# Transposes of split weights in high and low halves, other engines for the rests, and another order of the work

## The chip, the cores and the metric

The kernel runs on one core of one Trainium2 chip. The metric is the device time of one execution in microseconds (us); a time "before" is the median of several runs of the unchanged kernel. One further execution was profiled, and the rows in this document come from it.

The core has a tensor engine (TensorE, PE in the rows; PEld is its weight load), VectorE (DVE), ScalarE (ACT), GpSimd (POOL) and SyncE (SP), which here only issues DMAs. Each engine works through its own instructions in the order of the program and waits at semaphores for the others.

## The reference

Stage 1 is attention over a window of 64 positions; stage 2 is a mixture of four experts, each a causal attention, of which every position uses two:

```python
# stage 1: batch 8, 8 heads, 576 positions, 64 columns a head
scores = scale * np.matmul(q, k.transpose(0, 1, 3, 2))
mask = (rel >= 0) & (rel < 64)
attn = softmax(np.where(mask, scores, -1e9))      # sum + 1e-9 below the line
x = concat_heads(np.matmul(attn, v))              # 8 x 576 x 512
# stage 2: 4 experts, 64 columns each, the 2 largest logits a position
logits = x @ w_gate
for e in range(4):
    q, k, v = x @ wq[e], x @ wk[e], x @ wv[e]
    a = softmax(causal(scale * (q @ k.transpose(0, 2, 1))))
    out += chosen_weight[e] * (a @ v @ wo[e])
```

## The kernel before

Everything is float32 at the ends and is computed with numbers split into a high and a low part, so that the products of the parts keep the accuracy.

**Stage 1** goes over 72 groups of four tiles: scores (`s1_mm`, m in the order), mask and softmax (`s1_qk`, q; the norms are GpSimd's line 338), transposes on TensorE (`s1_t`, t; line 361) and products with v (`s1_av`, a).

**Stage 2** goes over the eight batches b and, in each, over two pairs pr of experts. Per batch: values (`s2_v`, v: the result is split into three bf16 parts `V2`, the second and third made from a rest by two GpSimd instructions each, lines 510 and 511), gate (`s2_gate`, g) and output (`s2_o`, o). Per (b, pr): projections (`s2_k`, k; `s2_q`, r), scores (`s2_mm`, x, line 601), softmax (`s2_soft`, y), and then the part that the change is about:

- `s2_w` (u, lines 645 to 670) makes nine rows of weights, row x belonging to block (x+1)//2 of the causal pattern: 64, 192, 192, 320, 320, 448, 448, 576 and 576 columns. ACT writes the high part in f16 (line 663). The low part is the rest: by one VectorE instruction (line 666) or by two GpSimd instructions, multiply and subtract (lines 668, 669). `LOW` says which: rows 0 to 6 by GpSimd and rows 7 and 8 by VectorE; in the last pair (7,1) `LAST` gives all to VectorE. `u..0` has rows 0 to 6, `u..1` rows 7 and 8.
- `s2_turn` (D, line 678) turns the split weights by a DMA transpose from the source tile `SPLIT` (sp) to `TURN` (tu), issued by SP. k = 0 takes blocks 0 to 2 (22 tiles of 128 x 128, "blocks" in what follows of a DMA's size), k = 1 block 3 (16), k = 2 block 4 (20). High and low parts lie together and go in one DMA. Blocks 3 and 4 share `SPLIT[1]`: block 4 is written when block 3 has been read; in between GpSimd clears a strip of it (line 480).
- `s2_av` (A, line 701) multiplies the turned weights with `V2`: part 0 (k = 0) in 50 matmuls, part 1 (k = 1 and 2) in 60, for each piece of the pattern the five products of parts one behind the other: three with the high weights, two with the low ones. ACT and VectorE split the result into `YH` and `YL` (lines 708, 710), from which `s2_o` makes the output.

**The order** is written out by hand: the string `ORDER` lists the units; each naming runs the unit to its next `yield`, and the digits behind a colon are the PSUM banks it takes. Each engine receives its instructions in that order and keeps it. SP thus issues loads (p and h), transposes (D) and stores (the last step of o) in one queue: a transpose that waits for its weights holds all that stand behind it.

A unit is named with its indices: D712 is batch 7, pair 1, k = 2; A710 is batch 7, pair 1, part 0. The last pair stands like this in the order (`...` leaves out):

```python
... x710:31 x710 k711 k711 x712:46 x712 x711:27 x711 u701
... D702 D702 o54 o54 o60 o60 u710 u710 u710 ... y713 y713 y713
u711 o61:7 A700:2 o62:4 A701:6 o61 o63:5 o62 D710 D710 D711 D711 o61 o61 o62 o62 u711 A710:3 A710 u711 u711
u711 u711 u711 o63 A701 A700 A701 A710 A710 A700 A700 o71:1 o70:7 D712 D712 ... A711:4 A711 A711 o72:5 ...
```

Of the kernel before, what the change touches and what calls it, by code (L numbers as in the profile page):

```python
# [30 lines left out]
LOW = "PPPPPPPDD"  # L31
LAST = "DDDDDDDDD"
# [127 lines left out]
def window_attention_moe_attention(ctx: ExitStack, tc: tile.TileContext, qT, kT, vW,  # L160
# [264 lines left out]
    def place(i, e, low):  # L425

        if i == 0:
            return 0, low, low
        n = i + 1
        at = (0, 2, 10, 0, 0)[i] + n * (2 * low + e)  # L430
        return int(i > 2), at, at + (16 if i == 4 else 0)

# [409 lines left out]
```

## Time and profile before

| what | value |
|---|---|
| median of 3 runs | 504.77 us (503.76 to 505.1) |
| profiled execution, whole time | 502.08 us |
| its span, first to last instruction | 500.4 us |
| instructions | 16956 |
| TensorE busy | 445.5 us (89%), 6192 matmuls |
| VectorE busy | 418.4 us (84%) |
| ScalarE busy | 356.5 us (71%) |
| GpSimd busy | 303.6 us (61%) |
| transposes `tu<-sp` | 48, median 5.7 us from issue to landing |

The time is the whole execution's, the span what lies between its first and last instruction; rows count from the span's start. A share of busy time says how much of a stretch an engine worked, and nothing on what it waited for: that is told by the number in brackets behind a row (idle time ahead of it, and what ended it) and by the chain of waits, which follows the work that ended last back to the start. "To landing" is the time from a DMA's issue to the semaphore that tells of its end.

### The profile page before, as it was taken

How to read it: one execution, taken by the hardware profiler on the slowest of the kernel's cores; microseconds unless marked ns; L12 is line 12 of the kernel's file. 1: busy time of each engine (PE TensorE's matmuls, PEld its weight loads, DVE VectorE, ACT ScalarE, POOL GpSimd, SP SyncE). 2: the span in 40 equal slices, each digit the busy share in tenths (PEclk: the TensorE clock that was granted, in tenths of full speed). 3: DMA queues.
4: the chain of work that ended last, by engine and by line, in shares of the span. 5: the costliest groups of instructions: out<-in, count | busy, mean ns of one | idle time of the engine just before them, and what ended most of it. 6: DMA issues, size and time to landing. Idle time of an engine off the chain costs nothing.

```text
span 500.4 us, 16956 instructions
## 1 busy us (share of the span) xinstructions
PE 445.5 (89%) x6192; PEld 395.2 (79%) x6192; DVE 418.4 (84%) x1788; ACT 356.5 (71%) x1304; POOL 303.6 (61%) x663
## 2 busy tenths in 40 slices
PE   7999998797899797999789899989999989978846
PEld 6788888686798676978689888879888879967735
DVE  5879999898799997989979999989999896882720
ACT  6987997486775676768877588758696677574642
POOL 6987597767474763574748364967659364764000
PEclk9999999999899998999989999998999989998979
DMA  8954373849895597095976679494996675466684
GB/s 270 372 215 149 101 203 94 162 92 198 173 162 160 124 222 256 1 224 121 210 229 127 169 175 184 128 153 96 270 193 125 169 122 102 78 141 125 144 162 141
DMA packets 141251, 81.85 MB, mean 164 GB/s; under 512 B 123120, under 2 KB 124144, under 8 KB 141168
## 3 DMA queue, kind: packets, MB, share of 16 engines
q1 hardware_dynamic: 141088, 80.63, 68.7%
q8 instruction: 49, 0.80, 0.7%
q14 instruction: 34, 0.28, 0.2%
q10 hardware_dynamic: 80, 0.13, 0.1%
HBM read 40.90 MB, written 9.44 MB: 101 GB/s over the span
## 4 chain that ended last, share of the span: by engine, by line
DVE 34%; DMA 22%; PE 16%; POOL 12%; ACT 9%; issue 6%; SPq 1%; POOLq 0%; DVEq 0%; ACTq 0%
DMA tu<-sp 18%; DVE p L616 6%; DVE pt L375 5%; DVE sm L314 4%; POOL p L338 4%; PE ps L701 4%; ACT sm L325 4%; DVE sp L666 2%; PE ps L487 2%; DVE p L322 2%; DMA k<-in_kT_dram 2%; PE ps L601 2%; PE ps L488 2%; PE ps L489 2%; ACT sp L663 2%
## 5 line engine op out<-in xcount | busy, mean ns | idle before, releaser
L338 POOL TENSOR_SCALAR p<-p,st 128x64 f32<-128x64 f32 x216 | 73.0, 361 | 40.0 <-DVE st L334 20.1
L663 ACT ACTIVATE sp<-p,r 128x576 f16<-128x576 f32 (+3 forms) x128 | 72.3, 607 | 31.4 <-DMA tu<-sp 22.1
L620 ACT ACTIVATE p<-p,r 128x192 f32<-128x192 f32 (+3 forms) x128 | 77.2, 606 | 19.9 <-DVE r L616 14.7
L325 ACT ACTIVATE p<-p,st 128x64 f32<-128x64 f32 x216 | 72.3, 338 | 10.7 <-DVE p L322 8.4
L701 PEld LDWEIGHTS <-v 128*64 128x64 bf16 x1760 | 61.0, 113 | 22.6 <-issue 13.2
L701 PE MATMUL ps<-tu,v 128*64 128x64 f16 (+2 forms) x1760 | 64.0, 232 | 16.6 <-DMA tu<-sp 9.6
L375 DVE TENSOR_TENSOR pt<-ps,tri 64x512 f32<-64x512 f32 (+1 forms) x120 | 75.4, 632 | 3.5 <-PE ps L361 1.8
L669 POOL TENSOR_TENSOR sp<-p,sp 128x192 f16<-128x192 f32 (+2 forms) x90 | 72.3, 804 | 7.5
L616 DVE CUSTOM_DVE_ANT_0 p<-ps,causal 128x320 f32<-128x320 f32 (+3 forms) x160 | 67.9, 469 | 4.3 <-PE ps L601 2.5
L314 DVE CUSTOM_DVE_ANT_0 sm<-ps,win 128x128 f32<-128x128 f32 x264 | 61.8, 281 | 5.9 <-PE ps L297 4.9
L601 PE MATMUL ps<-kt,qt 64*128 64x256 f32 (+2 forms) x480 | 50.5, 333 | 6.5 <-DVE kt L571 2.0
L668 POOL TENSOR_SCALAR p<-p,r 128x192 f32<-128x192 f32 (+2 forms) x90 | 51.4, 571 | 4.7 <-ACT sp L663 4.7
L297 PE MATMUL ps<-k,q 64*64 64x128 f32 (+1 forms) x1080 | 41.6, 279 | 8.6 <-DMA k<-in_kT_dram 6.1
L601 PEld LDWEIGHTS ps<-kt,qt 64*128 64x128 f32 x480 | 36.9, 190 | 13.4 <-DVE kt L571 2.5
L388 PE MATMUL ps<-pt,v 128*64 128x64 f32 x1080 | 38.7, 226 | 5.3 <-DMA v<-in_vW_dram 2.5
L297 PEld LDWEIGHTS ps<-k,q 64*64 64x64 f32 x1080 | 31.8, 137 | 14.4 <-issue 4.8
L487 PE MATMUL ps<-xh,wqhi 128*128 128x320 f32 (+1 forms) x128 | 40.2, 314 | 2.8 <-ACT out L178 1.1
L388 PEld LDWEIGHTS ps<-pt,v 128*64 128x64 f32 x1080 | 34.5, 139 | 10.2 <-DMA v<-in_vW_dram 2.8
L325 ACT ACTIVATION_READ_ACCUMULATOR p<-p,st 128x1 f32 x216 | 41.2, 191 | 0.0
L480 POOL MEMSET sp<- 128x256 f16 (+1 forms) x35 | 10.7, 309 | 49.6 <-DMA tu<-sp 43.5
L487 PE MATMUL ps<-xh,wkhi 128*128 128x256 f32 (+1 forms) x128 | 39.7, 310 | 0.9 <-DVE kt L571 0.8
L666 DVE SCALAR_TENSOR_TENSOR sp<-p,r,sp 128x576 f16<-128x576 f32 (+3 forms) x38 | 31.0, 830 | 11.1 <-ACT sp L663 10.8
(138 smaller groups left out, 1283.8 us busy)
## 6 DMA issues: line engine op xcount, KB each, us to landing
v<-in_vW_dram SPq DMA_DIRECT2D x30, 576.0 KB, 4.9
k<-in_kT_dram SPq DMA_DIRECT2D x29, 320.0 KB, 4.4
q<-in_qT_dram SPq DMA_DIRECT2D x29, 288.0 KB, 4.1
out_dram<-out SPq DMA_DIRECT2D x32, 256.0 KB, 3.9
out_dram<-out SPq DMA_DIRECT2D x7, 128.0 KB, 2.5
tu<-sp SPq DMA_TRANSPOSE x48, 5.7
sp<-in_kT_dram SPq DMA_DIRECT2D x2, 320.0 KB, 6.4
p<-in_qT_dram SPq DMA_DIRECT2D x2, 288.0 KB, 5.7
```

Of the source, the lines that this page charges most:

```text
L297: nc.tensor.matmul(S1[g][i][o:o + 64, c:], lhsT=q_t[r, 64 * b:64 * b + 64], rhs=k_t[r, 64 * b + c:64 * b + 128], start=True, stop=True)
L314: nc.vector.tensor_tensor_reduce(out=to, in0=ps[i][:, c:], in1=win[:, int(b == 0), c:], scale=-0.125, scalar=3.0e38, op0=OP.add, op1=OP.mi ...
L325: nc.scalar.activation(pt[:, i], pt[:, i], AF.Exp, bias=st[:, 0, z + i:z + i + 1], scale=-1.0, accum_out=st[:, 1, z + i:z + i + 1])
L338: nc.gpsimd.tensor_scalar(p, p, st[:, 2, i:i + 1], 1.0, op0=OP.mult, op1=OP.mult)
L375: nc.vector.tensor_mul(t[64 * w:64 * w + 64, :n, e], ps[r, :n], tri[r, w, None, :].to_broadcast([64, n, 128]))
L388: nc.tensor.matmul(o[64 * h:64 * h + 64, 4 * x + i], lhsT=pairs[p][2][:, h, b], rhs=t[:, i, c:c + 64], start=True, stop=True)
L487: nc.tensor.matmul(ps, lhsT=ah, rhs=bh, start=first, stop=False)
L601: nc.tensor.matmul(ps[e][:, at(i):at(i) + n], lhsT=QT[pr][r, w, q], rhs=KT[b, pr][r, m, key:key + n], start=x == 0, stop=x == 2)
L616: nc.vector.tensor_tensor_reduce(out=dst, in0=src, in1=mask, scale=1.0, scalar=3.0e38, op0=OP.add, op1=OP.min, accum_out=to)
L620: nc.scalar.activation(p, p, AF.Exp, bias=r2[:, 0, x:x + 1], scale=-1.0, accum_out=r2[:, 1, x:x + 1])
L663: nc.scalar.activation(hi, p, AF.Copy, scale=by)
L701: nc.tensor.matmul(to, lhsT=V2[b % 2][:, c, a, 2 * pr + h], rhs=rhs, start=n == 0, stop=n == len(work_list) - 1, skip_group_check=True)
```

## The change

`ORDER` is replaced as a whole, and six places of the code with it:

1. A turn becomes two DMAs, one for the high and one for the low part: D gets a fourth index (0 high, 1 low), `place` lays all high parts of a turn side by side and all low parts behind them, and sizes halve to 11, 8 and 10 blocks.
2. `s2_av` goes over the five products outside and over the pieces of the pattern inside: all products with high weights come first.
3. Rows 7 and 8 get their rests from GpSimd too; from (6,1) on, so in (6,1), (7,0) and (7,1), VectorE makes all nine.
4. The second and third parts of `V2` of the last batch are made by VectorE.
5. `clear_split` follows the new places.
6. The units get another order and other banks.

```diff
-LOW = "PPPPPPPDD"
-LAST = "DDDDDDDDD"
+LOW = "PPPPPPPPP"
+LATE = (6, 1)
...
     def place(i, e, low):
-        if i == 0:
-            return 0, low, low
-        n = i + 1
-        at = (0, 2, 10, 0, 0)[i] + n * (2 * low + e)
-        return int(i > 2), at, at + (16 if i == 4 else 0)
+        if i < 3:
+            at = 11 * low + (0, 1 + 2 * e, 5 + 3 * e)[i]
+            return 0, at, at
+        at = 2 * low * (i + 1) + e * (i + 1)
+        return 1, at, at + (16 if i == 4 else 0)
...
     def clear_split(i):
-        x, at, _ = place(i, 0, 0)
-        n, c = (4, i + 1) if i else (2, 1)
-        t = SPLIT[x].bitcast(F16)[:, 128 * at:128 * (at + n * c)].rearrange("r (a c) -> r a c", a=n)
-        nc.gpsimd.memset(t[:, :, 128 * c - 64:], 0.0)
+        for low in range(1 if i > 2 else 2):
+            x, at, _ = place(i, 0, low)
+            n, c = (1 if i == 0 else 2 if i < 3 else 4), i + 1
+            t = SPLIT[x].bitcast(F16)[:, 128 * at:128 * (at + n * c)].rearrange("r (a c) -> r a c", a=n)
+            nc.gpsimd.memset(t[:, :, 128 * c - 64:], 0.0)
...
-            nc.gpsimd.tensor_scalar(dst[1], rest, 1.0, 1.0, op0=OP.mult, op1=OP.mult)
-            nc.gpsimd.tensor_tensor(dst[2], rest, dst[1], op=OP.subtract)
+            engine = nc.vector if b == NB - 1 else nc.gpsimd
+            engine.tensor_scalar(dst[1], rest, 1.0, 1.0, op0=OP.mult, op1=OP.mult)
+            engine.tensor_tensor(dst[2], rest, dst[1], op=OP.subtract)
...
-            if (LAST if (b, pr) == (NB - 1, 1) else LOW)[x] == "D":
+            if LOW[x] == "D" or (b, pr) >= LATE:
                 nc.vector.scalar_tensor_tensor(lo, p, by, hi, op0=OP.mult, op1=OP.subtract)
...
-    def s2_turn(b, pr, k):
-        n = (22, 16, 20)[k]
-        src = SPLIT[int(k > 0)].bitcast(F16)[:, 0:128 * n]
-        at = (0, 0, 16)[k]
-        to = TURN[int(k > 0)].bitcast(F16)[:, 128 * at:128 * (at + n)]
-        nc.sync.dma_start_transpose(to.rearrange("r (a c) -> r a c", a=n), src)
+    def s2_turn(b, pr, k, low):
+        n = (11, 8, 10)[k]
+        x, at, to = place((0, 3, 4)[k], 0, low)
+        src, dst = (t[x].bitcast(F16)[:, 128 * a:128 * (a + n)] for t, a in ((SPLIT, at), (TURN, to)))
+        nc.sync.dma_start_transpose(dst.rearrange("r (a c) -> r a c", a=n), src)
...
-        work_list = [(c, blocks, q, q0, a, low) for c, blocks, q, q0 in AVS[part] for a, low in PRODUCTS]
+        work_list = [(c, blocks, q, q0, a, low) for a, low in PRODUCTS for c, blocks, q, q0 in AVS[part]]
```

The end of the new order, from the stretch of batch 6's last transposes on (`...` leaves out; a transpose is named twice, its second naming does nothing):

```python
... y700 A600 ... A601:6 D6110 D6110 D6111 D6111 D6101 D6101 x701:13 x701
... k710:5 r710:4 o53:2 r711:3 ... x702:17 x702 ... D6120 D6120 ... A610:2 D6121
D6121 x703:17 x703 x710:45 x710 o54:3 ... D7000 D7000 A611:1 ... k711:7 k711 ... o60:2 ... D7001 D7001
x712:34 x712 k711 k711 x711:57 x711 y711 D7010 D7010 D7011 D7011 u701 ...
D7020 D7020 D7021 D7021 x713:27 x713 o63:5 o61:1 o62:6 y711 y711 u710 u710 u710 u710 u710 u710 u710 u710
u710 o61 u710 u710 u710 u710 A700:1 y712 y712 y713 A701:3 o61 o61 D7101 D7101 u710 o62 u710
y713 y713 D7110 D7110 u711 u710 u710 D7111 D7111 u711 u711 A700 u711 u711 D7100 D7100 A701 A701 A700 A700
A701 A701 A701 u711 u711 D7120 D7120 D7121 D7121 o62 o62 A710:6 A710 o63 A710 A710 o70:4 ... o71:2 ... A711:7 ...
```

## Rows read from the trace of the kernel before

**Rows 1.** The page: busy us (share of the span) and instructions of an engine.
```profile
PE 445.5 (89%) x6192; PEld 395.2 (79%) x6192; DVE 418.4 (84%) x1788; ACT 356.5 (71%) x1304; POOL 303.6 (61%) x663
```

**Rows 2.** Stretches: length, busy us (instructions) of PE, PEld, DVE, ACT, POOL; clock, DMA.
```profile
60.00:440.00 380.00, 346.61 (x4869) 311.32 (x4865) 344.31 (x1409) 274.99 (x1012) 246.52 (x523) 0.98 0.71 157
440.00:462.00 22.00, 17.22 (x185) 15.21 (x183) 11.82 (x47) 13.24 (x37) 11.97 (x20) 0.92 0.59 123
462.00:500.40 38.40, 26.33 (x314) 20.98 (x312) 14.42 (x48) 17.90 (x45) 0.93 (x3) 0.88 0.65 150
484.00:488.00 4.00, 3.60 (x8) 2.65 (x9) 1.42 (x5) 0.57 (x3) 0.00 (x0) 0.50 0.68 130
492.00:496.00 4.00, 4.00 (x24) 3.44 (x22) 0.58 (x2) 1.39 (x4) 0.00 (x0) 1.00 0.22 81
350.00:375.00 25.00, 24.27 (x377) 21.33 (x374) 24.53 (x103) 19.71 (x72) 14.35 (x31) 1.00 1.00 234
400.00:425.00 25.00, 23.42 (x250) 21.76 (x249) 19.60 (x74) 17.98 (x57) 13.77 (x27) 0.93 0.63 112
```

**Rows 3.** The chain of waits from 440 us on: its shares by engine and line.
```profile
by line: DMA tu<-sp 44.9%; PE ps L701 12.5%; issue 6.1%; DVE sp L666 4.8%; DMA out_dram<-out 3.3%; DVE p L616 3.0%; PE ps L487 2.9%; ACT sp L663 2.3%; PE ps L488 2.0%; PE ps L489 1.9%; PE ps L601 1.7%; POOL px L668 1.2%; POOL sp L669 1.2%; 
```

**Rows 4.** Pieces of that chain: start us, length us, what.
```profile
439.92 4.25 DMA tu<-sp
...
472.66 7.29 DMA tu<-sp
...
484.38 4.86 DMA tu<-sp
```

**Rows 5.** SP's transposes: two timeline rows, all 48 (ns), and the landing of D711.
```profile
472.66 3.63 SPq L678 DMA_TRANSPOSE tu<-sp  x1
...
476.45 2.98 SPq L678 DMA_TRANSPOSE tu<-sp  x1
...
L678 SPq DMA_TRANSPOSE tu<-sp x48: 1317/3275/8168, 69.9 to 484.4; - x48
...
DMA to landing us min/median/max: 5.1/5.1/5.1
```

**Rows 6.** Timeline from 462 us: start, length, engine, line, operation, shapes [idle before <-releaser].
```profile
462.06 2.10 PE L601 MATMUL ps<-kt,qt 64*128 64x256 f32 x24
...
472.57 2.42 PE L701 MATMUL ps<-tu,v 128*64 128x256 f16 x60 [1.43 <-DMA tu<-sp]
...
479.99 1.53 PE L701 MATMUL ps<-tu,v 128*64 128x256 f16 x50 [3.40 <-DMA tu<-sp]
484.40 0.80 PE L487 MATMUL ps<-wohi,yh 128*128 128x512 f32 x1 [2.88 <-ACT yh L708]
...
489.28 2.42 PE L701 MATMUL ps<-tu,v 128*64 128x256 f16 x60
...
472.46 1.23 ACT L663 ACTIVATE sp<-p,r 128x448 f16<-128x448 f32 x2 [1.07 <-DMA tu<-sp]
...
470.16 1.81 DVE L666 SCALAR_TENSOR_TENSOR sp<-p,r,sp 128x192 f16<-128x192 f32 x4
```

**Rows 7.** Groups by line and shape: xcount | busy us, mean ns of one | idle before.
```profile
L669 POOL TENSOR_TENSOR sp<-p,sp 128x448 f16<-128x448 f32 x30 | 31.3, 1045 | 2.5
...
L666 DVE SCALAR_TENSOR_TENSOR sp<-p,r,sp 128x576 f16<-128x576 f32 x32 | 27.9, 883 | 9.8 <-ACT sp L663 9.6
...
L669 POOL TENSOR_TENSOR sp<-p,sp 128x320 f16<-128x320 f32 x30 | 24.4, 813 | 2.5
...
L668 POOL TENSOR_SCALAR p<-p,r 128x448 f32<-128x448 f32 x30 | 19.9, 663 | 2.1 <-ACT sp L663 2.1
...
L668 POOL TENSOR_SCALAR p<-p,r 128x320 f32<-128x320 f32 x30 | 16.6, 553 | 1.3 <-ACT sp L663 1.3
```

**Rows 8.** Waits: who for whom, us in total, times, longest.
```profile
POOL sp L480 <- DMA tu<-sp: 43.5, 12, 8.8
...
PE ps L361 <- POOL p L338: 3.6, 5, 1.4
```

More of the change, by code (lines that the diff above doesn't have):

```diff
@@ L777, in window_attention_moe_attention @@
             for k in range(3):
-                unit(f"D{b}{pr}{k}", s2_turn, b, pr, k)
+                for low in range(2):
+                    unit(f"D{b}{pr}{k}{low}", s2_turn, b, pr, k, low)
             for k in range(4):
```

240 rows, old and new, of the table ORDER are left out of this document.

## The prediction

> **What bounds the kernel now.** I read the busy shares first: TensorE is busy 445.5 of 500.4 us, VectorE 418.4 [rows 1], two engines close together. An average hides stages, so the second view is busy time by stretch [rows 2]. From 60 to 440 us TensorE (346.6 of 380 us) and VectorE (344.3) are tied, each free for a tenth of the time, and GpSimd has room (246.5). After 440 us this is over: from there to 462 TensorE works 17.2 of 22 us, and in the last 38.4 us, from the scores of the last head pair on, it works 26.3, so 12.1 us hold no matmul. Third, the chain of waits over that last stage: 44.9% of it is the transposes that turn the split weights (`tu<-sp`), against 12.5% for the products that use them [rows 3]. So the end of the kernel is a latency chain, the middle is a contest of TensorE and VectorE, and the change touches both.
>
> The chain at the end, in order of time: D710 is issued at 472.66 and holds SP's queue for 3.63 us; D711 behind it goes out at 476.45 and lands 5.1 us later, at about 481.5 [rows 4, 5]. Block 4 shares its source tile with block 3, so its parts wait for that landing; D712 goes out at 484.38 and lands at 489.24 [rows 4]. TensorE meanwhile waits 1.43, 3.40 and 2.88 us [rows 6]. Behind these waits the granted clock is 0.50, the lower of its two levels, from 484 to 488 us; from 492 us on, with matmuls back to back, it is 1.00 [rows 2].
>
> **The halves of the transposes.** The 48 DMAs become 96, over the same bytes. D611, of 16 blocks, lands after 4.25 us, D712, of 20, after 4.86 us [rows 4]: 0.15 us a block, and 1.85 us that do not depend on size. By that line a half of 8, 10 or 11 blocks lands after 3.05, 3.35 or 3.5 us. No row shows a half; the bounds are half of the 16-block landing (2.1 us) and all of it (4.25 us), and I take the line, since both its points are undisturbed issues and the nearer is only 1.5 times larger. On SP's queue the shortest of the 48 took 1.32 us, the median 3.275, and D711 2.98 [rows 5]; a half should not cost more than the shortest whole one, and I take 1.3, between 0.7 and 2.0 us: 96 of them hold SP for 125 us, where 48 at the median hold it for 157. The size-free part overlaps when two are issued back to back: D710 landed at 479.95, and D711, issued 3.8 us after it, 1.6 us later [rows 4, 5].
>
> The Trainium skill, DMA: Bandwidth & Descriptors, section "Anatomy of one DMA", gives every transfer a fixed cost of about 2.0 us, and its rules for kernel authors tell you to coalesce small transfers. The trace agrees on the fixed part (1.85 us); were the 48 added DMAs to pay those 2.0 us one after another, the sum would lose 96 us, and the overlap just shown speaks against that.
>
> What is moved: behind a transpose that waits in SP's queue stand the loads of later pairs and the stores of outputs, and a low half now waits there as a whole one did before. In the order as written the two halves mostly stand together, and in the last pair the low half D7101 even stands ahead of D7110 and D7100. The gain is therefore that each part is short, that block 4's first high part can be written once block 3's high parts have been read, and that the products wait in the order high, low.
>
> **The last 38 us.** I take the trace's own clock as a ruler. The new D7020 needs two high parts and no rests; it goes out and lands sooner, so ACT's wait of 1.07 us at 472.46 [rows 6] goes. D7101 leaves SP at about 472.4; D7110 has to wait for A701's high products, which end near 473.9, and D7111 follows at 475.2 and lands 3.05 us later, at 478.2, where D711 landed at 481.5. Between that landing and D712's issue lay 2.9 us for two high parts and their rests; the high half waits for the second high part alone, which I put 0.9 us after the landing. D7120 goes out near 479.1 and D7121 1.3 us behind it, landing near 483.8 instead of 489.24: 5.4 us earlier. TensorE now becomes what is late. From the last scores at 462.06 to A711 at 489.28 [rows 6] it spent 27.2 us, of which 7.7 were the three waits and about 1.6 the low clock (four us at 0.50, less the waiting in them), so 17.9 us of work. The new order puts three more units behind those scores: A611 (60 products like those at 472.57, 2.42 us [rows 6]), o54 and k711 (18 matmuls, 3.0 us at 24 in 4.00 us [rows 2]). That makes 23.3 us of work against a chain of 21.8. Loss before, 9.3 us; loss after, some 2 us for the wait before A710. So 7 us are won, with 3 and 9 as bounds (3: the chain stays and only the added units fill it).
>
> **From 440 to 462 us.** TensorE is free 4.8 us there [rows 2]. In the new order six of its units (x701, k710, r710, o53, r711, x702) stand between the last transpose that A610 needs and A610; before, none did. I take 1.5 us, between 0 and 4.
>
> **The middle.** VectorE loses the rests of rows 7 and 8 for 13 head pairs: 26 x 0.883 = 23.0 us [rows 7], 6.7% of what it does there. It gets back later, where it has room, the 14 rests of (6,1) and (7,0): the last pair's rows 1 to 4, 1024 columns, took 1.81 us [rows 6], a pair's seven have 1984, so 3.5 us a pair, 7.0 us; and the four late rests of v, eight instructions of 256 columns, 3.1 us by the columns of rows 7, no more than 7. GpSimd gets 26 x 2.05 = 53 us: multiply and subtract cost 553 and 813 ns at 320 columns, 663 and 1045 at 448 [rows 7], hence 773 and 1277 at 576. It goes from 246.5 to 300 of 380 us, 79%. So one of two tied engines is relieved, and a third gets dense. What does that give to TensorE? It is free for 33 us there and will hardly win more than 10; a GpSimd that comes late can cost it 8. I take 2 us won, near zero, because a less busy VectorE does not go with a busier TensorE in this trace: 24.53 and 24.27 of 25 us from 350 us, 19.60 and 23.42 from 400 us [rows 2]. The order of products changes nothing in their number, and the moved columns of `place` nothing in the memsets: as many of the same kind.
>
> **Sum.** 7 + 1.5 + 2 = 10.5 us. The profiled execution took 502.08 us (span 500.4 and 1.7 around it); it would take 491.6. The median of the runs shown, 504.77, lies 2.7 us above the profiled one, and I take the gain from it: 494.3 us.
>
> **Rivals.**
> GpSimd becomes the bound of the middle (slower). A pair's two long rests take 4.1 us on it instead of 1.8 on VectorE, and it works in order: behind them stand the norms (L338), for which the transposes L361 already wait 3.6 us, and the memsets, which hold it 43.5 us until a transpose has landed [rows 8]. It decides from where the low half, moved by 2.3 us, lands past the TensorE work that the order puts between D and A; that is several units, but the norms have no such cover. If half the 13 pairs lose 2.3 us and the norms as much again, that is 30 us; if half of this reaches TensorE, 504.8 - 8.5 + 15 = 511. Against it: a fifth of GpSimd's time is still free.
> A half costs nearly as much as a whole. At 4.25 us each the end's chain keeps 2 to 3 us more, and the DMA engines, 0.71 busy in the middle [rows 2], come near 1, so that loads come late: gain at the end 4, loss in the middle 10 or more, 511.
> The gain stays at the end and the middle gives part of it back: 504.8 - 8.5 + 4 = 500.3.
> It does not do what it says: halves issued side by side land together, high products first then save nothing, and the order wins back only one of the waits: 503.5.
> The middle wins as much as VectorE's relief could bring: 504.8 - 8.5 - 10 = 486.
>
> **How the numbers follow.** About 0.3% (1.5 us) is what a measurement of this kernel can tell from no change. Chances: the forecast with its own bounds, 489 to 498, 0.50; middle gives back 0.18; relief in full 0.05; no effect 0.09; GpSimd the bound 0.13; dear halves 0.05. Faster: 0.50 + 0.18 + 0.05 and 0.02 of the no-effect case = 0.75; within 0.3%: 0.08, the rest of that case and a little of the two losing ones; slower 0.17. The range takes in the relief case and the milder part of the two losing ones, and leaves out the rest of these: 486 to 506.
>
> **What would show it.** In the trace after: halves that land in 3.0 to 3.6 us with SP held for 1.3 or less (right), or above 4 (the second rival). In the last 38 us less than 7 us without a matmul, and a granted clock of 1.00 up to the last product. In the middle VectorE near 321 us, GpSimd near 300, and TensorE's free time about 31 us; if it grew, with waits of L361 on L338 or of SP on GpSimd's rests ahead, GpSimd has become the bound and I was wrong about the middle. I am wrong about the end if TensorE still waits for `tu` there by more than 2 us.

## The result, and the profile after

| | before | after |
|---|---|---|
| median of 4 runs each | 504.45 us (503.76 to 505.1) | 484.57 us (483.19 to 485.02) |
| ratio, with its 95% interval | 1 | 0.9601 [0.9576, 0.9627] |
| profiled execution, span | 500.4 us | 483.3 us |
| TensorE without a matmul in the span | 54.9 us | 38.8 us |

The changed kernel is 19.9 us, 4.0%, faster. The prediction had the sign right and the size wrong: it said 494.3 us, with 486 to 506 as its range, and the time lies below that range.

The page of the kernel after, its busy line and the shares of its chain of waits by engine, and behind them the same shares of the kernel before:

```profile
PE 444.5 (92%) x6192; PEld 391.7 (81%) x6192; DVE 423.9 (88%) x1784; ACT 357.2 (74%) x1304; POOL 323.9 (67%) x682
...
DVE 56%; PE 21%; POOL 7%; issue 5%; DMA 5%; ACT 4%; SPq 1%; DVEq 0%; POOLq 0%; ACTq 0%
```

```profile
DVE 34%; DMA 22%; PE 16%; POOL 12%; ACT 9%; issue 6%; SPq 1%; POOLq 0%; DVEq 0%; ACTq 0%
```

The busy line answers to [rows 1]. TensorE's work is the same (444.5 against 445.5 us), so what was won is idle time of TensorE: 16.1 us of the span's 17.1. GpSimd works 20 us more, and VectorE, which the change was to relieve, works 5.5 us more than before. VectorE now holds 56% of the chain, where it held 34%, and DMA 5%, where it held 22%.

To see where the 16.1 us came from, the next rows begin with the first scores of all (x000, at 49.1 us before and 47.4 after; ahead of them TensorE idles 4.6 and 4.7 us) and take as a border the first scores of batch 7 (x700), which both kernels compute. Columns as in [rows 2]. First the kernel after: up to x700, from x700 on, from x710 on, and one stretch near the end; then the kernel before, up to x700 and from there on:

```profile
47.40:422.70 375.30, 353.06 (x4976) 314.04 (x4976) 355.76 (x1461) 286.45 (x1059) 285.17 (x582) 0.99 0.75 163
422.70:483.30 60.60, 48.73 (x629) 41.60 (x625) 34.21 (x127) 33.30 (x89) 1.56 (x5) 0.87 0.71 146
439.00:483.30 44.30, 32.44 (x394) 26.91 (x390) 20.20 (x67) 21.85 (x55) 1.25 (x4) 0.86 0.72 153
466.00:470.00 4.00, 4.00 (x45) 3.33 (x42) 0.78 (x2) 0.93 (x2) 0.00 (x0) 0.50 1.17 162
```

```profile
49.10:431.90 382.80, 350.00 (x4892) 314.48 (x4892) 348.05 (x1458) 281.87 (x1045) 245.26 (x528) 0.98 0.70 155
431.90:500.40 68.50, 51.06 (x640) 42.78 (x636) 32.83 (x118) 35.02 (x93) 19.56 (x33) 0.91 0.66 144
```

| TensorE idle, us | before | after | won |
|---|---|---|---|
| from x000 to x700 | 382.80 - 350.00 = 32.8 | 375.30 - 353.06 = 22.2 | 10.6 |
| from x700 on | 68.50 - 51.06 = 17.4 | 60.60 - 48.73 = 11.9 | 5.5 |
| of that, from x710 on | 38.40 - 26.33 = 12.1 [rows 2] | 44.30 - 32.44 = 11.9 | 0.2 |

Two thirds were won in the middle, where the prediction expected 2 us, and next to nothing after x710, where it expected 7.

The chain of waits from 60 to 440 us, by line, tells what went out of the middle. Before:

```profile
by line: DMA tu<-sp 17.1%; DVE p L616 6.7%; DVE pt L375 6.6%; POOL p L338 5.7%; issue 5.7%; DVE sm L314 4.3%; PE ps L701 3.2%; DMA k<-in_kT_dram 2.9%; DVE p L322 2.8%; PE ps L487 2.4%; DVE sp L666 2.3%; PE ps L488 2.2%; PE ps L489 2.2%; POO
```

After:

```profile
by line: DVE pt L381 14.9%; DVE p L624 9.5%; DVE sm L320 6.7%; issue 5.2%; DVE p L328 4.8%; PE ps L609 4.1%; DVE xl L405 3.4%; PE ps L708 3.3%; DVE vr L515 2.8%; PE ps L494 2.1%; PE ps L496 1.9%; POOL p L344 1.8%; PE ps L495 1.8%; PE ps L39
```

The transposes were 17.1% of that chain, its largest entry. After, they are not among the entries shown; VectorE's lines 381, 624 and 320 lead. The waits for `tu` in the whole run say who was held up: columns are who for whom, us in total, times, longest. Before, then after:

```profile
ACT sp L663 <- DMA tu<-sp: 22.1, 12, 3.8
...
PE ps L701 <- DMA tu<-sp: 9.6, 6, 3.4
```

```profile
POOL sp L487 <- DMA tu<-sp: 32.7, 6, 9.2
...
PE ps L708 <- DMA tu<-sp: 6.7, 1, 6.7
ACT sp L671 <- DMA tu<-sp: 6.2, 5, 2.2
```

ScalarE's wait with the next high part for a source tile that is still being read falls from 22.1 to 6.2 us. GpSimd's wait with the memsets goes from 43.5 [rows 8] to 32.7.

### The profile page after: what moved, and what is told of

It is laid out like the page before. It is cut to its first block, busy times and chain, and to the rows that moved or that the text cites. A ratio compares the mean times of both kernels' runs of the same rounds, so it can differ in the third digit from the quotient of the medians.

```text
span 483.3 us, 17081 instructions
## 1 busy us (share of the span) xinstructions
PE 444.5 (92%) x6192; PEld 391.7 (81%) x6192; DVE 423.9 (88%) x1784; ACT 357.2 (74%) x1304; POOL 323.9 (67%) x682
## 4 chain that ended last, share of the span: by engine, by line
DVE 56%; PE 21%; POOL 7%; issue 5%; DMA 5%; ACT 4%; SPq 1%; DVEq 0%; POOLq 0%; ACTq 0%
DVE pt L381 12%; DVE p L624 8%; DVE sm L320 6%; PE ps L708 4%; PE ps L609 4%; DVE p L328 4%; DMA k<-in_kT_dram 3%; DVE xl L405 3%; PE ps L494 3%; PE ps L394 2%; PE ps L496 2%; DVE vr L515 2%; PE ps L495 2%; ACT p L628 2%; PE ps L303 2%
## 5 line engine op out<-in xcount | busy, mean ns | idle before, releaser
L677 POOL TENSOR_TENSOR sp<-p,sp 128x192 f16<-128x192 f32 (+3 forms) x104 | 96.8, 931 | 8.7
L628 ACT ACTIVATE p<-p,r 128x192 f32<-128x192 f32 (+3 forms) x128 | 77.2, 607 | 21.9 <-DVE r L624 15.0
L344 POOL TENSOR_SCALAR p<-p,st 128x64 f32<-128x64 f32 x216 | 64.3, 322 | 32.4 <-DVE st L340 17.8
L671 ACT ACTIVATE sp<-p,r 128x192 f16<-128x192 f32 (+3 forms) x128 | 72.3, 609 | 9.2 <-DMA tu<-sp 6.2
L676 POOL TENSOR_SCALAR p<-p,r 128x192 f32<-128x192 f32 (+3 forms) x104 | 63.0, 606 | 17.1 <-ACT sp L671 17.1
L624 DVE CUSTOM_DVE_ANT_0 p<-ps,causal 128x320 f32<-128x320 f32 (+3 forms) x160 | 67.8, 470 | 4.3 <-PE ps L609 2.6
L609 PE MATMUL ps<-kt,qt 64*128 64x256 f32 (+2 forms) x480 | 54.3, 333 | 7.8 <-DVE kt L579 2.4
L494 PE MATMUL ps<-xh,wkhi 128*128 128x320 f32 (+1 forms) x128 | 39.7, 310 | 1.5 <-DVE st L320 0.7
L494 PE MATMUL ps<-xh,wqhi 128*128 128x256 f32 (+1 forms) x128 | 39.3, 307 | 1.5 <-DVE yl L717 0.8
L487 POOL MEMSET sp<- 128x256 f16 (+2 forms) x38 | 10.7, 291 | 44.4 <-DMA tu<-sp 32.7
L496 PE MATMUL ps<-xh,wqlo 128*128 128x256 f32 (+1 forms) x128 | 37.8, 296 | 0.0
```

The source lines that it names most:

```text
L494: nc.tensor.matmul(ps, lhsT=ah, rhs=bh, start=first, stop=False)
L609: nc.tensor.matmul(ps[e][:, at(i):at(i) + n], lhsT=QT[pr][r, w, q], rhs=KT[b, pr][r, m, key:key + n], start=x == 0, stop=x == 2)
L624: nc.vector.tensor_tensor_reduce(out=dst, in0=src, in1=mask, scale=1.0, scalar=3.0e38, op0=OP.add, op1=OP.min, accum_out=to)
L628: nc.scalar.activation(p, p, AF.Exp, bias=r2[:, 0, x:x + 1], scale=-1.0, accum_out=r2[:, 1, x:x + 1])
L671: nc.scalar.activation(hi, p, AF.Copy, scale=by)
L677: nc.gpsimd.tensor_tensor(lo, p, hi, op=OP.subtract)
```

## The experiments

A ratio below is to the kernel before in the same group of runs, with its 95% interval. Kernels whose names begin with "old" keep the order of the kernel before, those with "new" the order of the kernel after.

### The halves alone, in the old order

```diff
 # kernel after, with
-LOW = "PPPPPPPPP"
-LATE = (6, 1)
+LOW = "PPPPPPPDD"
+LATE = (7, 1)
-            engine = nc.vector if b == NB - 1 else nc.gpsimd
+            engine = nc.gpsimd
-ORDER = (the new order)
+ORDER = (the old order, each Dxyz named as Dxyz0 Dxyz0 Dxyz1 Dxyz1)
```

> The kernel before, in its own order and with its own engines for the rests, but with each transpose replaced in its place by a high and a low half and with the products in the order high, low. After the first four runs (523.1 us for all new code in the old order, 520.7 for the old code in the new order, 510.5 for the new kernel with whole transposes, 495.9 with the long rests back on VectorE) two accounts are left. 'Halves are worth something in any order': 493 to 500 us here, and the loss of the first run comes from the long rests on GpSimd alone. 'Halves need an order made for them': 502 to 508 us, about as before, since the whole next step still waits for the low half in the old places.

Measured: 493.41 us, ratio 0.9754 [0.9718, 0.9789], inside the 493 to 500 us of the account by which halves are worth something in any order. Halves, and the places and the order of products that go with them, give 2.5%, some 12 us, with nothing else changed. The two stretches, divided at x700 as above, and the chain and the waits of this kernel:

```profile
51.00:429.60 378.60, 351.86 (x4893) 314.77 (x4894) 352.56 (x1458) 281.83 (x1045) 246.82 (x531) 0.98 0.73 158
429.60:491.70 62.10, 50.76 (x638) 42.21 (x636) 32.81 (x118) 35.08 (x93) 19.47 (x33) 0.93 0.75 153
...
by line: DVE pt L381 8.1%; DVE p L624 7.4%; issue 6.8%; DMA tu<-sp 6.0%; DVE sm L320 5.9%; DVE sp L674 4.5%; DVE p L328 3.5%; DMA k<-in_kT_dram 3.2%; PE ps L494 2.8%; DMA v<-in_vW_dram 2.7%; PE ps L708 2.6%; PE ps L496 2.6%; PE ps L495 2.6%
...
ACT sp L671 <- DMA tu<-sp: 4.7, 3, 2.5
...
PE ps L708 <- DMA tu<-sp: 1.9, 2, 1.7
```

TensorE idles 378.60 - 351.86 = 26.7 us up to x700 and 62.10 - 50.76 = 11.3 from there on: 6.1 us won in each. So the 5.5 us that the change wins at the end are there without the new order, and more than half of what it wins in the middle comes from the halves too. The transposes' share of the chain falls from 17.1 to 6.0%, ScalarE's wait from 22.1 to 4.7 us, while VectorE's work (422.9 us by the page, against 418.4) and GpSimd's (305.4, against 303.6) hardly change.

### Whole transposes in the changed kernel

```diff
-    def s2_turn(b, pr, k, low):
-        n = (11, 8, 10)[k]
-        x, at, to = place((0, 3, 4)[k], 0, low)
+    def s2_turn(b, pr, k):
+        n = (22, 16, 20)[k]
+        x, at, to = place((0, 3, 4)[k], 0, 0)
-ORDER = (the new order)
+ORDER = (the new order, one D in the place of the later of its two halves)
```

> The changed kernel with only the halves undone: one transpose for high and low parts at the place of the later of the two. Theory 'halves': 493 us or more, and transposes back on the chain with over 12% of the span. Theory 'order' or 'relief': 484 to 488 us, some us at most for the transposes that go out later.

Measured: 510.48 us (505.97 to 511.51), ratio 1.0065 [1.0027, 1.0104]. Without the halves the changed kernel is 26 us slower than with them and 0.65% slower than the kernel before. Its waits for `tu`, from the quickest of its executions:

```profile
ACT sp L664 <- DMA tu<-sp: 34.0, 13, 6.0
...
PE ps L701 <- DMA tu<-sp: 10.7, 2, 9.9
```

34.0 us of ScalarE and 10.7 of TensorE, against 6.2 and 6.7 after. The time is what the account by halves expected; the share of the chain is not: the transposes hold 6.9% of it, against over 12% expected. Without the halves nothing is left of the gain. The same holds of the new order, as the tables below show.

### Halves without the early release of the source tile

In the changed kernel the first of block 4's two high parts lies where block 3's high half is read, so it can be written before the low half has landed; the second reaches into the low half's place (blocks 5 to 9, where the low half begins at 8). Here block 4's high parts are laid where block 3's low half is read, and its low parts where the high half is read. The DMAs, their sizes and the order stay; ScalarE must wait for the low half before it can write the first high part too.

```diff
-        at = 2 * low * (i + 1) + e * (i + 1)
-        return 1, at, at + (16 if i == 4 else 0)
+        to = 2 * low * (i + 1) + e * (i + 1)
+        if i == 4:
+            return 1, 10 * (1 - low) + 5 * e, to + 16
+        return 1, to, to
...
             x, at, _ = place(i, 0, low)
+            at = 0 if i == 4 else at
```

> As the run with halves in the old order (493.41 us, 12 us below the kernel before), with one edit: block 4's high and low parts change places in the shared source tile, so that its high parts lie over block 3's low ones and wait for the low half's landing; sizes, order and products stay. 'Halves pay because the shared tile comes free earlier' (ACT's waits for tu fell from 22.1 to 4.7 us): 497 to 503 us, ACT waiting 10 us or more for tu. 'Halves pay because each transpose and each issue is shorter': 493 to 495 us.

> The same edit in the changed kernel: block 4's high parts wait for block 3's low half. With whole transposes in this order the time was 510.48 us and ACT waited 34.0 us for tu, after the change 6.2 us. 'Earlier release': 490 to 500 us. 'Shorter transposes': 484 to 487 us.

Measured: 496.99 us, 0.9815 [0.9758, 0.9872], in the old order, and 500.43 us, 0.9879 [0.9806, 0.9952], in the new one. Each lies within half a microsecond of the range of the account by early release (497 to 503 and 490 to 500 us). ScalarE's wait, in the old order and then in the new:

```profile
ACT sp L674 <- DMA tu<-sp: 13.8, 9, 3.8
```

```profile
ACT sp L674 <- DMA tu<-sp: 22.0, 8, 6.3
```

In the new order the early release carries most of the gain: without it 1.2% are left of 4.0%, and ScalarE's wait is 22.0 us again. In the old order its effect (0.9754 to 0.9815) is not separated, since the intervals overlap; there the halves give 1.85% without it, and at least 1.3% by the interval. ScalarE's wait is 13.8 us there, against 22.1 before. So in the old order most of the 2.5% is there without the early release, and which property of the halves gives it, the shorter transposes or the earlier issue of what stands behind them, no run here divides.

### The rests of rows 7 and 8, and the order

Four kernels with halves and four without make two tables. Rests of rows 7 and 8 by VectorE:

```diff
 # kernel after, with
-LOW = "PPPPPPPPP"
+LOW = "PPPPPPPDD"
```

> The changed kernel with rows 7 and 8 on VectorE again for the 13 head pairs up to (6,0); everything else as after. Theory 'relief': 490 us or more. Theories 'order' and 'halves': 484 to 488 us. VectorE was busy 5.5 us more after the change although 26 rests had left it, its small instructions being longer; if GpSimd's density is what lengthens them, they get shorter here (the 128x7 product of L660 back from 421 ns towards 167 ns) and VectorE's busy time rises by less than the 23 us put back.

Rests by GpSimd in the old order, as the whole new code and as one edit of the old:

```diff
 # kernel after, with
-ORDER = (the new order)
+ORDER = (the old order, each Dxyz named as Dxyz0 Dxyz0 Dxyz1 Dxyz1)
```

> All changed code, in the old order of the work: each old transpose is replaced in its place by its high half and, right behind it, its low half; nothing else is moved. The result to be explained is 504.45 us before and 484.57 us after. Theory 'order' (the new order places more work between a transpose and its use): 502 to 507 us, as before. Theory 'halves' (short transposes and products in the order high, low take the transposes off the chain by themselves): 488 to 493 us. Theory 'relief' (VectorE freed of 26 long rests): 494 to 499 us.

```diff
 # kernel before, with
-LOW = "PPPPPPPDD"
+LOW = "PPPPPPPPP"
```

> The kernel before with one edit: rows 7 and 8 get their rests from GpSimd in all pairs but the last. In the run with all new code in the old order VectorE waited 15.0 us in ten waits of its masks (L624) for GpSimd's rests (L677), which still read the tile that it overwrites. If this is what the old order cannot bear: 515 to 525 us. If VectorE's relief counts: below 500 us. If the two cancel: 502 to 508 us.

And the old code in the new order:

```diff
 # kernel before, with
-ORDER = (the old order)
+ORDER = (the new order, one D in the place of the later of its two halves)
```

> The old code in the new order: whole transposes, each at the later of its two halves' places, old order of products, long rests on VectorE again, all rests of v on GpSimd. Theory 'order': 485 to 489 us. Theory 'halves': 498 us or more. Theory 'relief': 492 to 497 us. If both this kernel and the one with the new code in the old order lie above 497 us, order and code gain only together.

| with halves, us | old order | new order |
|---|---|---|
| rests of rows 7, 8 by VectorE | 493.41 | 495.88, 0.9807 [0.9744, 0.987] |
| rests of rows 7, 8 by GpSimd | 523.05, 1.0345 [1.0286, 1.0403] | 484.57 |

| whole transposes, us | old order | new order |
|---|---|---|
| rests of rows 7, 8 by VectorE | 504.45 | 520.74, 1.0287 [1.0229, 1.0345] |
| rests of rows 7, 8 by GpSimd | 550.22, 1.0874 [1.0834, 1.0913] | 510.48 |

GpSimd's long rests cost 30 us in the old order with halves and 45 without; both times lie beyond every range that had been expected for them. In the new order the same rests win some 10 us in either case. The new order by itself wins nothing: with halves its 0.9807 can't be told from the 0.9754 of the old order, and without them it loses 15 us. Each needs the other. (Some neighbours in the tables also differ in the late rests and in the order of products; the next two experiments find no effect of these, with halves, in one order each.)

What GpSimd's rests hold up in the old order is seen in the waits, first of the old code with the one edit, then of the new code in the old order:

```profile
ACT sp L663 <- DMA tu<-sp: 50.4, 19, 7.8
...
DVE p L616 <- POOL sp L669: 22.3, 13, 3.9
PE ps L701 <- DMA tu<-sp: 21.9, 8, 5.8
...
PE ps L361 <- POOL p L338: 9.5, 11, 3.7
```

```profile
DVE p L624 <- POOL sp L677: 15.0, 10, 4.0
```

VectorE's masks of the next pair (L616, or L624 in the new code) write the tile that GpSimd's rests are still reading: 22.3 and 15.0 us, an entry that neither the kernel before nor the kernel after has. The norms that the transposes on TensorE wait for go from 3.6 us [rows 8] to 9.5. In the new order no such wait of the masks is listed. In the old code the waits for the transposes grow most: ScalarE's from 22.1 to 50.4 us, TensorE's from 9.6 to 21.9. A whole transpose goes out only when GpSimd's rests are written, and the chain of that kernel shows it, with GpSimd at 28% where it held 12%:

```profile
POOL 28%; DMA 22%; DVE 19%; PE 16%; issue 9%; ACT 4%; SPq 1%; POOLq 0%; ACTq 0%; DVEq 0%
```

With halves ScalarE's wait stays at 6.3 us in the old order, and the masks' wait is the new one. How the 30 and 45 us divide among these waits is not shown.

The upper and the lower kernel of the new order with halves say what VectorE's relief was worth. Its instructions on a few columns, grouped by line and shape as in [rows 7]: before, after, and the new order with the long rests on VectorE:

```profile
L546 DVE COPY g<-gt 64x2 f32<-64x2 f32 x16 | 2.9, 180 | 0.2
...
L652 DVE TENSOR_TENSOR r<-r,g 128x7 f32<-128x7 f32 x16 | 2.7, 167 | 0.6
```

```profile
L677 POOL TENSOR_TENSOR sp<-p,sp 128x576 f16<-128x576 f32 x26 | 33.6, 1291 | 2.2
...
L676 POOL TENSOR_SCALAR p<-p,r 128x576 f32<-128x576 f32 x26 | 20.8, 799 | 11.9 <-ACT sp L671 11.9
...
L660 DVE TENSOR_TENSOR r<-r,g 128x7 f32<-128x7 f32 x16 | 6.7, 421 | 0.6
...
L554 DVE COPY g<-gt 64x2 f32<-64x2 f32 x16 | 5.6, 349 | 0.2
```

```profile
L674 DVE SCALAR_TENSOR_TENSOR sp<-p,r,sp 128x576 f16<-128x576 f32 x32 | 25.7, 823 | 11.1 <-ACT sp L671 7.6 <-DMA tu<-sp 3.4
...
L554 DVE COPY g<-gt 64x2 f32<-64x2 f32 x16 | 3.4, 214 | 0.2
...
L660 DVE TENSOR_TENSOR r<-r,g 128x7 f32<-128x7 f32 x16 | 2.8, 174 | 0.6
```

The product of two tiles in SBUF of 7 columns takes 167 ns before, 421 after, and 174 when GpSimd doesn't make the long rests. The mean of 421 hides two kinds. Of the 16 products after, four take 0.94 to 1.10 us and the others 0.17 to 0.43. Each of the four begins while GpSimd subtracts a rest of 576 columns and ends within 0.03 us of that subtraction; from VectorE's timeline one of them and one product beside which GpSimd does nothing, and from GpSimd's the subtraction:

```profile
103.78 1.04 DVE L660 TENSOR_TENSOR r<-r,g 128x7 f32<-128x7 f32 x1
...
132.10 0.17 DVE L660 TENSOR_TENSOR r<-r,g 128x7 f32<-128x7 f32 x1
```

```profile
103.51 1.29 POOL L677 TENSOR_TENSOR sp<-p,sp 128x576 f16<-128x576 f32 x1
```

It is a matter of when the two meet: with the same long rests in the old order the mean is 221 ns without halves and 233 with them.

26 of the third kernel's 32 rests of 576 columns went to GpSimd, 25.7 - 4.7 = 21.0 us of VectorE's work (the remaining 6 take 4.7 us after), yet its busy time is only 428.7 (by its page) - 423.9 = 4.8 us above the kernel after. The rest of the relief was taken back by longer instructions: 3.9 us by the product, 2.2 by the copy, and the remainder by others, at most 2.2 us each. The Trainium skill, SBUF — State Buffer, section "Who interferes with whom", says that a VectorE instruction with two inputs in SBUF contends with GpSimd instructions that read SBUF, and that copies and scalar operations contend with it in their two-port modes. The traces agree for the product, in the four that end with the subtraction beside them, and the means of the three kernels agree for the copy of 64x2 (180, 349, 214 ns).

### The late rests

```diff
 # the halves in the old order, with
-LATE = (7, 1)
+LATE = (6, 1)
-            engine = nc.gpsimd
+            engine = nc.vector if b == NB - 1 else nc.gpsimd
```

> As the run with halves in the old order (493.41 us), with the late rests moved as the change does: all rests of (6,1) and (7,0) on VectorE, and the second and third parts of v of the last batch too; rows 7 and 8 stay on VectorE everywhere. If VectorE has room late (it was busy 26 of the last 60 us) and its one instruction of 0.55 to 0.68 us is shorter than GpSimd's two of 1.3 to 1.7: 490 to 493 us. If the late edits are neutral: 492.5 to 494.5 us. If they fall into VectorE's dense stretch before the last pair: 494.5 to 498 us.

Measured: 494.25 us, 0.9757 [0.9697, 0.9818], against 0.9754 without them. Rests (6,1), (7,0) and of v by VectorE change nothing that can be measured there.

### The order of products

```diff
-        work_list = [(c, blocks, q, q0, a, low) for a, low in PRODUCTS for c, blocks, q, q0 in AVS[part]]
+        work_list = [(c, blocks, q, q0, a, low) for c, blocks, q, q0 in AVS[part] for a, low in PRODUCTS]
```

> The changed kernel with the products of a piece side by side again, so that the first pieces wait for the low half at once. If the order high, low matters in itself, TensorE waits longer for tu and the time is 486 to 491 us. If halves mostly land together well ahead of the products (in the new order other TensorE work stands between them almost everywhere): 484 to 486 us, no difference.

Measured: 483.58 us, 0.9575 [0.953, 0.9619]. No difference from the kernel after (0.9601 [0.9576, 0.9627]) can be told.

### The high half D7100 ahead of D7101

```diff
-... o61 o61 D7101 D7101 u710 ... A700 u711 u711 D7100 D7100 A701 ...
+... o61 o61 D7100 D7100 D7101 D7101 u710 ... A700 u711 u711 A701 ...
```

> The changed kernel with one move in the order: the high half D7100 goes out ahead of the low half D7101 instead of behind D7111. In the trace after, TensorE waits 6.68 us for D7100 (issued 461.53, landed 465.15), the longest wait of the end. My account of the end: D7100 lands near 460 us, A710 and o70, o71 go 5 us sooner, and A711 then waits for D7121 near 471 us instead of starting at 472.26: 1 to 2 us won, 482.5 to 483.5 us. If the chain through D7111 and block 4 decides the end alone, the move delays D7111 by an issue of 1.3 us and the time is 484.5 to 486 us.

Measured: 484.51 us (480.95 to 487.59), 0.9565 [0.9521, 0.961]. TensorE's timeline of this kernel at A710 and behind it:

```profile
459.30 0.97 PE L707 MATMUL ps<-tu,v 128*64 128x256 f16 x30 [0.88 <-DMA tu<-sp]
463.07 0.71 PE L707 MATMUL ps<-tu,v 128*64 128x256 f16 x20 [2.80 <-DMA tu<-sp]
465.16 0.80 PE L493 MATMUL ps<-wohi,yh 128*128 128x512 f32 x1 [1.38 <-ACT yh L714]
```

The wait ahead of A710, 6.68 us after, becomes 0.88 and 2.80 (the low half now lands late, at 463.03), and waits of 1.38 and 0.45 us for o70's input come in. That is 5.5 us of idle time in the place of 6.7. Products then start 5.9 us earlier (459.30 against 465.19), but A711 only 1.2 us earlier (471.05 against 472.26), and block 4 is not turned sooner (its low half lands at 471.07, against 470.44). In the medians nothing of this is seen.

## Why the prediction was wrong

**The price of a half: right.** All 96 transposes of the kernel after, as in [rows 5]:

```profile
L685 SPq DMA_TRANSPOSE tu<-sp x96: 1231/1380/4725, 60.0 to 466.3; - x96
...
DMA to landing us min/median/max: 3.0/3.7/8.8
```

The quickest landings were 3.04 us for 8 blocks, 3.33 for 10 and 3.49 for 11; the line through two whole transposes had given 3.05, 3.35 and 3.5. SP was held 1.38 us by a half (median), where 1.3 was put. In sum SP was held 151.5 us by the halves against 167.4 by the whole ones, not 125 against 157: some halves hold SP far longer, up to 4.7 us, and a median doesn't see them. The rival of dear halves falls. The Trainium skill, DMA: Bandwidth & Descriptors, section "Rules for kernel authors", says to coalesce small transfers; this kernel does not bear that out for transfers of 8 to 11 blocks (256 to 352 KB): with 48 more DMAs, and nothing else but their places and the order of products, the time fell by 2.5%. The fixed cost of 2.0 us that the prediction took from the Trainium skill, DMA: Bandwidth & Descriptors, section "Anatomy of one DMA", is given there for DMAs that GpSimd issues; those here are issued by SP, and their quickest landings show 1.85 us.

**The middle: the step that failed.** The prediction gave the halves' gain to the last 38 us and none to the middle; there it weighed only VectorE's relief against GpSimd's delay, and took 2 us. Measured are 10.6 us up to x700, and the halves alone give 6.1 of them. What gives the other 4.5 is not divided (see below). The failure is one of reading: the chain of waits was read for the last stretch [rows 3] and not for the stretch from 60 to 440 us, where 17.1% of it were transposes. The busy shares of [rows 2] were taken for a contest of TensorE and VectorE; they could not show that ScalarE and GpSimd waited there for the same shared source tile as at the end. Each of the 16 pairs has the same three transposes, not the last one alone.

**VectorE and GpSimd.** VectorE was to fall from 344 to near 321 us in the middle. In the stretch up to x700 it rose, from 348.05 to 355.76. The long rests did go, and what was moved cost GpSimd 1291 + 799 ns a row, against 1277 + 773 put. Over the whole run VectorE's rests fell from 31.3 to 15.9 us and the late parts of v added 4.0; its other 1749 instructions, the same number in both kernels, took 16.9 us longer. Of these the product of 7 columns was looked at one by one, and there it is the meeting with a GpSimd rest, which the prediction did not price. A relief of VectorE's busy time is thus not what brought the time near 486.

**GpSimd as the bound: the mechanism is real, its chance was not.** In the old order GpSimd's long rests lose 30 us with halves, the upper figure of that rival, and 45 without. Without halves the places are those of that rival and one more: the transposes that go out late (50.4 us of ScalarE's and 21.9 of TensorE's waiting), the norms (9.5), and VectorE's next masks (22.3), which wait for the tile that the rests read and which the prediction did not name. With halves the masks' wait is the new one (15.0). The prediction reckoned the order as it was written only for the end and gave it no credit for the middle, where no wait of the masks for the rests is left in the new order.

**The end: a gain of the right kind, at the wrong border.** 8.5 us were put for everything from 440 us on; 5.5 were won from x700 on, nearly all of it ahead of x710, and the same kind of gain (6.1) comes from the halves alone. The ruler began at x710, since in the kernel before the last scores x713 follow 3.9 us later (465.91). In the new order A611, o54, k711 and o60, which were to fill the waits, stand ahead of x713 (449.79, 10.8 us after x710, for all but the first of its six matmuls), so they delay the start of the chain instead. Counted from there, D7121 lands after 20.7 us (470.44) where D712 landed after 23.3 [rows 4], 2.6 us earlier, not 5.4; and A711 starts 22.5 us after x713 instead of 23.4 [rows 6], so of these 2.6 only 0.9 arrive (counted from x713's first matmul, at 448.45, none does). Three rows of TensorE, the two chain pieces that lead to A710, and SP's issues:

```profile
449.79 0.62 PE L609 MATMUL ps<-kt,qt 64*128 64x256 f32 x5 [0.96 <-DVE r L624]
...
465.19 2.61 PE L708 MATMUL ps<-tu,v 128*64 128x256 f16 x50 [6.68 <-DMA tu<-sp]
...
472.26 2.42 PE L708 MATMUL ps<-tu,v 128*64 128x256 f16 x60
...
460.25 1.23 SPq L685
...
461.53 3.61 DMA tu<-sp
...
456.24 11.44 SPq L685 DMA_TRANSPOSE tu<-sp  x6
```

Of the last pair's halves D7100 is issued fourth, at 461.53, after D7101, D7110 and D7111, so A710 waits 6.68 us, not "some 2"; and behind that wait, from 466 to 470 us, the granted clock is 0.50, not 1.00. By the test that the prediction set itself (more than 2 us of waiting for `tu`), it was wrong about the end. Moving D7100 up did not take that wait away: TensorE idled 5.5 us there instead of 6.7, and A711, which needs block 4, started 1.2 us earlier. What the end would gain without the wait is not shown.

**The order of products.** That it changes nothing in the number of products was right; that the products wait in the order high, low was counted as part of the gain, and is worth nothing that can be measured.

**The rival "relief in full", 486 us,** is the nearest in time. Its reason falls: VectorE's work did not go down.

**What stays open.** With halves, the change goes on from 493.4 to 484.6 us by long rests on GpSimd and the new order together. Of the mixed kernels one can't be told from the halves alone (495.9) and one loses (523.1), so these 9 us can't be divided between the two with the orders at hand; an order searched for VectorE's rests with halves would be needed, and was not tried. Nor was the early release tried by itself, as by a second source tile in the kernel before. No run is faster than the kernel after by more than the noise.

## What to carry to other kernels

Where one buffer is written, turned by a DMA and written again, try to split the DMA so that the first half frees the place that the next writer needs first: here halves gave 2.5% in an order not made for them, and in the order made for them most of the gain hung on when the place came free. Read the chain of waits for every stage, not only for the end: two engines near 90% busy hid a DMA that stood first in the chain. Work moved to an engine with time to spare needs an order made for it (30 us lost, or 11 won, by the same move), and the relieved engine's other instructions can grow longer where they meet the moved ones. An order has to be read at the instruction from which the chain really starts.

## What the runs showed of the hardware

- At its quickest, a transpose from SBUF to SBUF lands after about 1.85 us and 0.15 us a block of 128x128 f16, from 8 to 20 blocks (3.04, 3.33, 3.49 us for halves; 4.25 and 4.86 for whole ones [rows 4]); twice as many halves held SP for about the same time in sum (169.0 us in the old order, 151.5 after, 167.4 before).
- A VectorE product of two 128x7 tiles in SBUF that began within a GpSimd subtraction of 576 columns ended with it, after 0.94 to 1.10 us; with GpSimd idle it took 0.17 us. In the mean of 16 that made 421 ns after, and 174 ns in the same order without the long rests.
- The kernel whose TensorE waits most shows the most TensorE time for the same 6192 matmuls: 463.8 us at a mean granted clock of 0.938 in the kernel of 550.22 us, 444.5 at 0.973 after.
